# A different start order for a two-stage kernel: the first group alone up to its SSM block, and an input weight fetched ahead

## Chip, cores, metric

One NeuronCore of a Trainium2 (trn2) chip. The metric is device microseconds (us) of one execution; medians of several runs are given. "Warm" below means TensorE at its full clock, "cold" at half of it.

## The reference, cut to what matters

Two layers follow each other. All activations are float32; `moe_w_in` and `moe_w_out` arrive as float64.

```python
# gated linear attention, per batch b (4), head h (8), step t (768), head size 48
state = alpha[:, :, t, :, None] * state + einsum('bhd,bhe->bhde', k[:, :, t], v[:, :, t])
y[:, :, t] = einsum('bhd,bhde->bhe', q[:, :, t], state)
# gated SSM on x = y as (4, 768, 384)
proj = x @ w_in                       # (384, 1024): val | gate
h = exp(A_log) * h + val[:, t]        # scan over t
out = (silu(gate) * h) @ w_out        # (512, 384)
```

## The kernel before

The 4 x 768 steps are cut into N = 12 groups of 256 steps. A group passes through three generators; a `yield` ends a stage, and a schedule at the end decides which stage of which group is issued next. Each engine works through its instructions in the order in which they are issued.

- `front(n)`: transposes of alpha ("a"), scans V and P; transposes of q, product Q; of k, product K; scores `sc` and the masked copy A; K turned back (`tpk`, copies Kn). Five stages.
- `back(n)`: block states z and the running states S_n; y from inside a block; y from before it, then x_sb; x turned (xT). Four stages.
- `ssm(n)`: four blocks `pj` with scan `hh`, `sg` and `f`; two output products `o`. Six stages.

The float64 weights are turned into float32 by hand: 8 units of w_in and 4 of w_out. Step W(u) of `convert_weights` splits unit u and joins unit u-1.

```python
def split_unit(u):      # two ScalarE, two VectorE instructions, and on GpSimd:
    nc.gpsimd.tensor_scalar(out=ex, in0=ex, scalar1=896.0, scalar2=1151.0, op0=ALU.max, op1=ALU.min)
    nc.gpsimd.tensor_scalar(out=ex, in0=ex, scalar1=-896.0, scalar2=2.0 ** 23, op0=ALU.add, op1=ALU.mult)
def join_unit(u):
    nc.vector.scalar_tensor_tensor(out=ex, in0=hi, ...)
    nc.gpsimd.tensor_add(dst, dst, lo.bitcast(FP32))
    nc.gpsimd.tensor_mul(dst, dst, ex.bitcast(FP32))
def convert_weights():
    for u in range(len(units) + 1):
        if u < len(units):
            split_unit(u)
        if u > 0:
            join_unit(u - 1)
        yield

def back(n):            # (cut) first stage
    if not first:
        nc.gpsimd.tensor_mul(S_n[:, 0], S_end[0], ...)   # GpSimd, behind whatever W stands before it
    zv = block_states(s["Kn"], v_sb, ps_y)               # TensorE: z
    ...                                                  # VectorE: S_n, S_end from z
    yield

def ssm(n, ...):        # (cut) block cc needs units 2*cc (i = 0) and 2*cc + 1 (i = 1)
    for cc in range(NI):
        for i in range(2):
            for kk in range(NK):
                nc.tensor.matmul(pj[:, i, :], w_in[:, kk, i, ds(cc * C, C)], xT[:, kk, :], ...)
        # VectorE scan hh, ScalarE sg, VectorE f
        yield
```

The schedule of before, with `turn` the conversion for n < 3, and `old` and `new` the ssm of groups n-3 and n-2:

```python
for n in range(N + 3):
    # fr = front(n), ba = back(n - 1)
    step(fr); step(turn); step(ba); step(old); step(old); step(fr); step(turn); step(ba)
    # new = ssm(n - 2)
    step(new); step(fr); load(n + 2)          # n == 0: the rest of the weight fetches
    step(turn); step(ba); step(new); step(fr); step(ba); step(turn); step(new); step(fr); step(turn); step(new)
```

Of the kernel before, what the change touches and what calls it, by code (L numbers as in the profile page):

```python
# [18 lines left out]
def kernel(  # L19
# [38 lines left out]
    NI = DI // C  # L58
    N = B * NG
# [18 lines left out]
    def load_heads(dst, src, n, queue=nc.sync):  # L78

        b, g = divmod(n, NG)  # L80
        for c in range(G):
            rows = ds(g * GC + c * C, C)
            queue.dma_start(out=dst[:, c, :, 0:D], in_=src[b, :, rows, :].rearrange("h p d -> p h d"))  # L83

    def ssm(n, xT, prev_h, pool, ps_mm):

        b, g = divmod(n, NG)
        f = pool.tile([C, NI, GC], FP32, name="f")
        for cc in range(NI):
            pj = ps_mm.tile([C, 2, GC], FP32, tag="mm", name="pj")  # L90
            for i in range(2):
                for kk in range(NK):
                    nc.tensor.matmul(pj[:, i, :], w_in[:, kk, i, ds(cc * C, C)], xT[:, kk, :],  # L93
                                     start=(kk == 0), stop=(kk == NK - 1))
            hh = pool.tile([C, GC], FP32, tag=f"h{cc}", name="hh")
            nc.vector.tensor_tensor_scan(  # L96
                out=hh, data0=a_dec[:, cc:cc + 1].to_broadcast([C, GC]), data1=pj[:, 0, :],
                initial=prev_h[cc][:, GC - 1:GC] if g else 0.0, op0=ALU.mult, op1=ALU.add)
            prev_h[cc] = hh
            sg = pool.tile([C, GC], FP32, name="sg")  # L100
            nc.scalar.activation(sg, pj[:, 1, :], AF.Silu)  # L101
            nc.vector.tensor_mul(f[:, cc, :], sg, hh)  # L102
            yield
        for c in range(G):
            o = ps_mm.tile([C, DM], FP32, tag="mm", name="o")
            for cc in range(NI):
                nc.tensor.matmul(o, f[:, cc, ds(c * C, C)], w_out[:, cc, :],  # L107
                                 start=(cc == 0), stop=(cc == NI - 1))
            o_sb = pool.tile([C, DM], FP32, name="o_sb")
            nc.scalar.activation(o_sb, o, AF.Copy)  # L110
            nc.sync.dma_start(out=out[b, ds(g * GC + c * C, C), :], in_=o_sb)
            yield
# [9 lines left out]
    def block_states(Kn, v_sb, ps_y):  # L122

        z = ps_y.tile([C, NR, 512], FP32, tag="y", name="z")
        zv = z[:, :, 0:GP * D].rearrange("p r (g j e) -> p r g j e", g=G, e=D)
        for g in range(G):
            for j in range(NP):
                for r in range(NR):
                    for i in range(2):
                        rows, chs = ds(R * r, R), ds(DP * i, DP)  # L130
                        nc.tensor.matmul(zv[chs, r, g, j, :], Kn[rows, g, j, chs],
                                         v_sb[rows, g, 2 * j + i, :], start=True, stop=True,
                                         skip_group_check=True)
        return zv
# [32 lines left out]
    def features(x_sb, xT, ps_tp):  # L167

        for c in range(G):
            tp = ps_tp.tile([C, NK, C], FP32, tag="tp", name="tpx")  # L170
            for kk in range(NK):
                nc.tensor.transpose(tp[:, kk, :], x_sb[:, c, ds(kk * C, C)], ident)  # L172
            nc.scalar.activation(xT[:, :, ds(c * C, C)], tp, AF.Copy)

    def step(gen):
        if gen is not None:
            next(gen, None)


    def ranged(ctx):  # L180
        def pool(name, bufs, **kw):
            return ctx.enter_context(tc.tile_pool(name=name, bufs=bufs, **kw))
# [3 lines left out]
        p2 = pool("p2", 2)  # L186
# [6 lines left out]
        ps_mm = pool("ps_mm", 2, space=PS)  # L193
# [8 lines left out]
        vs, st, xs = {}, {}, {}  # L202

        def load(n, names="aqkv", queue=nc.sync):
            for name in names:
                if name == "v":
                    vs[n] = p3.tile([C, G, H, D], FP32, name="v_sb")
                dst = vs[n] if name == "v" else pads[n % NBUF][name]
                load_heads(dst, dict(a=alpha, q=q, k=k, v=v)[name], n, queue)
# [3 lines left out]
        units = []  # L213
# [8 lines left out]
        def fetch_unit(u, queue=nc.sync):  # L222
            dst, src = units[u]
            m, w = dst.shape[1:]
            bits = wst.tile([C, m, w, 2], U32, name=f"bits{u}")
            queue.dma_start(out=bits.rearrange("p a n two -> p a (n two)"), in_=src.bitcast(U32))  # L226
            words.append(bits)
# [24 lines left out]
# [7 lines that stand above are left out]
# [5 lines left out]
        prev_h = [None] * NI  # L264
# [75 lines left out]
        def back(n):  # L340

            s = st.pop(n)
            v_sb = vs.pop(n)
            first, last = n % NG == 0, n % NG == NG - 1
            S_n = p2.tile([C, GR, NP, D], FP32, name="S_n")
            if not first:
                nc.gpsimd.tensor_mul(S_n[:, 0], S_end[0], s["V"][:, :, 0:1].to_broadcast([C, NP, D]))  # L347
            zv = block_states(s["Kn"], v_sb, ps_y)
            S_end[0] = None if last else p2.tile([C, NP, D], FP32, name="S_end")
            for x in range(GR):  # L350
                src = zv[:, x % NR, x // NR]
                dst = S_n[:, x + 1] if x + 1 < GR else S_end[0]
                if first and x == 0:
                    nc.vector.tensor_copy(out=dst, in_=src)
                elif dst is not None:
                    nc.vector.tensor_add(dst, S_n[:, x], src)  # L356
            yield
            yv = values_inside(s["A"], v_sb, ps_y, p2)
            yield
            values_before(yv, s["Q"], S_n, first)  # L360
            x_sb = p2.tile([C, G, DM], FP32, name="x_sb")
            for i in range(2):
                nc.scalar.activation(x_sb.rearrange("p g (j i e) -> p i (g j) e", i=2, e=D)[:, i],
                                     yv[:, i].rearrange("p g j e -> p (g j) e"), AF.Copy)
            yield
            xs[n] = p2.tile([C, NK, GC], FP32, name="xT")
            features(x_sb, xs[n], ps_tp)
            yield

        ssms = {n: None for n in range(-3, N + 3)}  # L370
# [14 lines left out]
        load(0, "a")  # L385
        load(0, "q", nc.scalar)
        load(0, "k")
        fetch_unit(0)
        nc.scalar.dma_start(out=a_log, in_=moe_A_log.rearrange("(a p) -> p a", p=C))
        load(0, "v")  # L390
        fetch_unit(1)
        load(1, "aq")
        fetch_unit(2)
        load(1, "kv")
        for u in range(3, 6):
            fetch_unit(u)
        nc.scalar.activation(a_dec, a_log, AF.Exp)
        weights = convert_weights()

        def any_outside():  # L400
# [7 lines left out]
            nc.vector.tensor_reduce(out=w1, in_=wt, axis=mybir.AxisListType.X, op=ALU.max)  # L408
            nc.vector.tensor_scalar(out=flag, in0=w1, scalar1=0.0, scalar2=None, op0=ALU.is_gt)


        with tc.manual_schedule():
            for n in range(N + 3):
                fr = front(n) if n < N else None
                ba = back(n - 1) if 0 <= n - 1 < N else None
                old, new = ssms[n - 3], None
                turn = weights if n < 3 else None
                step(fr)
                step(turn)
                step(ba)  # L420
                step(old)
                step(old)
                step(fr)
                step(turn)
                step(ba)
                if 0 <= n - 2 < N:
                    new = ssms[n - 2] = ssm(n - 2, xs.pop(n - 2), prev_h, p2, ps_mm)
                step(new)
                step(fr)
                if n + 2 < N:  # L430
                    load(n + 2)
                if n == 0:
                    for u in range(6, len(units)):
                        fetch_unit(u)
                step(turn)
                step(ba)
                step(new)
                step(fr)
                step(ba)
                step(turn)  # L440
                step(new)
                step(fr)
                step(turn)
                step(new)
                if n == N:
                    any_outside()
                if n == N + 1:
                    outside = nc.values_load(flag[0:1, 0:1], min_val=0, max_val=1)
# [167 lines left out]
```

## Time and profile before

| | before |
|---|---|
| median of 4 runs | 374.15 us (373.93 to 374.33) |
| span of the profiled run | 372.8 us |
| TensorE busy | 325.8 us, 87% |
| VectorE, ScalarE, GpSimd busy | 54%, 29%, 15% |
| mean granted TensorE clock, as recorded | 0.975 |

In the profile PE is TensorE, PEld its weight loads, DVE VectorE, ACT ScalarE, POOL GpSimd and SP the engine that issues most DMAs. In the slices each digit is a busy share in tenths (9 is 90% or more), PEclk the granted TensorE clock in tenths; "out<-in xcount" names what a group of instructions writes and reads.

TensorE is full from about 66 us on. GpSimd is busy only 15% of the whole span, but nearly all of it lies in the first 70 us. The share of the span says nothing about that stretch.

Eight transposes of alpha took 1.94 us at 28.96, against 1.04 us at 87.48, and y took 3.65 us at 39.37, against 2.07 us at 96.07.

```profile
28.96 1.94 PE L294 MATMUL tp<-ident,a_pad 128*128 128x128 f32 x8 [7.17 <-POOL ex L240]
...
39.37 3.65 PE L145 MATMUL y<-v_sb,A 64*64 64x48 f32 x64 [1.60 <-DVE S_end L356]
```

### The profile page before, as it was taken

To read this page: it belongs to the slowest core of one execution; us is meant where nothing else is said; L and a number is where in the kernel's file an instruction comes from. 1 tells how busy PE (TensorE), PEld (TensorE's weight loads), DVE (VectorE), ACT (ScalarE), POOL (GpSimd) and SP (SyncE) were. 2 spreads that over 40 slices of the span, in tenths; PEclk is the share of its full clock that TensorE was granted. 3 is DMA by queue.
4 is the path that set the end of the run, shared out by engine and by line. 5 is a ranking of instruction groups with operands and counts; after the bars stand their busy time and mean duration, and the time that the engine had idled before them with its cause. 6 is when DMAs were issued, how large, how long until landed. Compare 5 with 4: busy or idle time off the path is not lost.

```text
span 372.8 us, 9626 instructions
## 1 busy us (share of the span) xinstructions
PE 325.8 (87%) x4233; PEld 265.6 (71%) x4233; DVE 200.5 (54%) x373; ACT 106.5 (29%) x231; POOL 56.8 (15%) x77
## 2 busy tenths in 40 slices
PE   2535851899999999999999999999999999999794
PEld 1425741787887886887887887878868868878582
DVE  3939785356557438348456555565484493403140
ACT  1414354221432323133223213223332231312111
POOL 4478898510000000000000000000000000000000
PEclk9999995599999999999999999999999999999999
DMA  9999992040470740911913704607401000010101
GB/s 132 212 220 190 303 171 47 2 86 2 105 111 2 154 60 3 179 36 41 145 30 80 134 2 100 115 3 130 85 2 44 2 16 30 2 45 0 38 7 50
DMA packets 107650, 29.02 MB, mean 78 GB/s; under 512 B 100944, under 2 KB 107088, under 8 KB 107600
## 3 DMA queue, kind: packets, MB, share of 16 engines
q1 hardware_dynamic: 104992, 27.93, 40.6%
q10 hardware_dynamic: 2608, 0.40, 0.9%
q8 instruction: 35, 0.57, 0.7%
q14 instruction: 15, 0.12, 0.1%
HBM read 23.60 MB, written 4.72 MB: 76 GB/s over the span
## 4 chain that ended last, share of the span: by engine, by line
PE 62%; DVE 23%; SPq 6%; issue 4%; POOL 2%; DMA 1%; ACT 1%; ACTq 0%; DVEq 0%; POOLq 0%
PE pj L93 35%; PE y L145 7%; DVE V L301 7%; DVE P L306 7%; PE o L107 4%; SPq L83 4%; PE y L163 4%; PE sc L331 3%; PE tp L294 3%; DVE S_n L356 3%; PE tpk L119 2%; PE tpx L172 2%; SPq L226 2%; DVE hh L96 2%; DMA bits<-in_moe_w_in_dram 1%
## 5 line engine op out<-in xcount | busy, mean ns | idle before, releaser
L93 PE MATMUL pj<-xT,w_in 128*128 128x256 f32 x576 | 136.1, 388 | 0.0
L93 PEld LDWEIGHTS pj<-xT,w_in 128*128 128x128 f32 x576 | 107.7, 193 | 14.6
L96 DVE TENSOR_TENSOR_SCAN hh<-a_dec,hh,pj 128x256 f32<-128x256 f32 x32 | 23.9, 747 | 78.2 <-PE pj L93 78.2
L107 PE MATMUL o<-w_out,f 128*128 128x384 f32 x192 | 65.0, 492 | 0.0
L101 ACT ACTIVATE sg<-pj 128x256 f32<-128x256 f32 x48 | 18.4, 383 | 130.9 <-DVE hh L96 130.9
L107 PEld LDWEIGHTS o<-w_out,f 128*128 128x128 f32 x192 | 35.5, 190 | 23.0 <-DVE f L102 0.5
L145 PE MATMUL y<-v_sb,A 64*64 64x48 f32 x768 | 28.0, 233 | 11.9 <-DVE S_end L356 11.2
L347 POOL TENSOR_TENSOR S_n<-S_end,V 128x192 f32<-128x192 f32 x8 | 4.1, 513 | 224.2 <-DVE S_end L356 224.2
L145 PEld LDWEIGHTS y<-v_sb,A 64*64 64x64 f32 x768 | 26.7, 149 | 15.1 <-issue 8.3
L306 DVE TENSOR_TENSOR_SCAN P<-tp,iV,bias 128x256 f32<-128x256 f32 x48 | 33.4, 738 | 0.8
L102 DVE TENSOR_TENSOR f<-sg,hh 128x256 f32<-128x256 f32 x48 | 20.4, 426 | 23.3 <-ACT sg L101 23.3
L301 DVE TENSOR_TENSOR_SCAN V<-tp,bias 128x256 f32<-128x256 f32 x48 | 30.1, 669 | 5.1 <-PE tp L294 5.1
L96 DVE TENSOR_TENSOR_SCAN hh<-a_dec,pj 128x256 f32<-128x256 f32 x16 | 11.0, 687 | 39.4 <-PE pj L93 39.4
L311 ACT ACTIVATE junk<-V,bias 128x1024 f32<-128x1024 f32 x12 | 13.8, 1148 | 52.7 <-DVE V L301 52.7
L294 PE MATMUL tp<-ident,a_pad 128*128 128x128 f32 x96 | 14.6, 300 | 15.6 <-POOL ex L240 7.2
L294 PE MATMUL tp<-ident,q_pad 128*128 128x128 f32 x96 | 15.5, 306 | 11.9 <-DVE P L306 7.7
L294 PEld LDWEIGHTS tp<-ident,a_pad 128*128 128x128 f32 x96 | 12.4, 154 | 17.4 <-POOL ex L240 7.5
L294 PEld LDWEIGHTS tp<-ident,q_pad 128*128 128x128 f32 x96 | 12.4, 157 | 16.4 <-issue 13.8
L240 POOL TENSOR_SCALAR ex<-ex 128x384 uint32<-128x384 uint32 x12 | 18.4, 1532 | 18.0 <-DVE ex L235 17.7
L331 PEld LDWEIGHTS sc<-Q,K 64*64 64x64 f32 x768 | 13.7, 144 | 4.3 <-issue 3.3
L334 DVE COPY_PREDICATED A<-mask,sc 128x512 f32<-128x512 uint8 x24 | 16.0, 721 | 1.1 <-PE sc L331 1.1
L322 DVE TENSOR_TENSOR K<-tp,V 128x512 f32<-128x512 f32 x24 | 15.5, 684 | 2.0 <-PE tp L294 2.0
(59 smaller groups left out, 315.6 us busy)
## 6 DMA issues: line engine op xcount, KB each, us to landing
a_pad<-in_alpha_dram SPq DMA_DIRECT2D x24, 192.0 KB, 4.7
k_pad<-in_k_dram SPq DMA_DIRECT2D x24, 192.0 KB, 5.1
v_sb<-in_v_dram SPq DMA_DIRECT2D x24, 192.0 KB, 5.0
out_dram<-o_sb SPq DMA_DIRECT2D x24, 192.0 KB, 2.1
q_pad<-in_q_dram SPq DMA_DIRECT2D x22, 192.0 KB, 5.0
bits<-in_moe_w_in_dram SPq DMA_DIRECT2D x8, 384.0 KB, 5.4
bits<-in_moe_w_out_dram SPq DMA_DIRECT2D x4, 384.0 KB, 6.1
q_pad<-in_q_dram ACTq DMA_DIRECT2D x2, 192.0 KB, 5.5
```

What stands on the lines that cost most here:

```text
L93: nc.tensor.matmul(pj[:, i, :], w_in[:, kk, i, ds(cc * C, C)], xT[:, kk, :], start=(kk == 0), stop=(kk == NK - 1))
L96: nc.vector.tensor_tensor_scan(out=hh, data0=a_dec[:, cc:cc + 1].to_broadcast([C, GC]), data1=pj[:, 0, :], initial=prev_h[cc][:, GC - 1:GC ...
L101: nc.scalar.activation(sg, pj[:, 1, :], AF.Silu)
L102: nc.vector.tensor_mul(f[:, cc, :], sg, hh)
L107: nc.tensor.matmul(o, f[:, cc, ds(c * C, C)], w_out[:, cc, :], start=(cc == 0), stop=(cc == NI - 1))
L145: nc.tensor.matmul(yv[rows, i, c, j, :], A[rows, i, c * NP + j, :], v_sb[rows, c, 2 * j + i, :], start=(c == 0 and j == 0), stop=False, sk ...
L240: nc.gpsimd.tensor_scalar(out=ex, in0=ex, scalar1=896.0, scalar2=1151.0, op0=ALU.max, op1=ALU.min)
L294: nc.tensor.transpose(tp[:, u, ds(c * C, C)], pad[name][:, c, 2 * j:2 * j + 2, :], ident)
L301: nc.vector.tensor_tensor_scan(out=V[:, 2 * jj + u, GC - 1::-1], data0=tp[:, u, ::-1], data1=bias[:, 1:2].to_broadcast([C, GC]), initial=1 ...
L306: nc.vector.tensor_tensor_scan(out=P[:, 2 * jj + u, :], data0=tp[:, u, :], data1=bias[:, 1:2].to_broadcast([C, GC]), initial=iV0[:, 2 * jj ...
L331: nc.tensor.matmul(scv[ds(R * r, R), i, c * NP + j, :], K[rows, j, steps], Q[rows, j, steps], start=True, stop=True, skip_group_check=True)
L334: nc.vector.copy_predicated(out=A[:, i].rearrange("p x t -> p (x t)"), mask=mask[:, ds(i * GP * R, GP * R)], data=sc[:, i])
```

## The change

Its intent: group 0 alone can reach its xT early. Then its pj blocks, TensorE work of some 11 us at full clock, can run in the holes that TensorE has while group 1 is at its scans and scores. For this the units of w_in must be there early, so they are fetched before group 1's inputs. The core of the diff (cut: comments and the branches that only keep other iterations as they were):

```diff
-        fetch_unit(0)
         nc.scalar.dma_start(out=a_log, ...)
         load(0, "v")
-        fetch_unit(1)
-        load(1, "aq")
-        fetch_unit(2)
-        load(1, "kv")
-        for u in range(3, 6):
+        for u in range(2 * NI):
+            fetch_unit(u)
+        load(1)
+        for u in range(2 * NI, len(units)):
             fetch_unit(u)
...
+            fr, ba = front(0), back(0)
+            for gen in (fr, fr, weights, fr, weights, fr, weights, fr, ba, weights, ba, ba, ba):
+                step(gen)
+            new = ssms[0] = ssm(0, xs.pop(0), prev_h, p2, ps_mm)
+            fr = front(1)
+            for gen in (fr, weights, new, fr, weights, new, fr, weights, weights, new, fr, weights, weights, new, fr):
+                step(gen)
+            load(2)
...
-            for n in range(N + 3):
+            for n in range(2, N + 3):
                 step(fr)
-                step(turn)
+                if n == 2:
+                    step(weights)
+                    step(weights)
                 step(ba)
...
-                if n + 2 < N:
-                    load(n + 2)
+                if n + 1 < N:
+                    load(n + 1)
...
+                step(old if n == 2 else new)     # n == 2: the o products of group 0, at two places
```

More of the change, by code (lines that the diff above doesn't have):

```diff
@@ L412, in ranged @@
         with tc.manual_schedule():
-            for n in range(N + 3):
-                fr = front(n) if n < N else None
-                ba = back(n - 1) if 0 <= n - 1 < N else None
-                old, new = ssms[n - 3], None
-                turn = weights if n < 3 else None
+            fr, ba = front(0), back(0)
[7 more added lines that the diff above has]
+            for n in range(2, N + 3):
+                fr = front(n) if n < N else None
+                ba = back(n - 1) if n - 1 < N else None
+                new = None
+                old = ssms[n - 3] if n > 2 else ssms[0]
+                if n == 2:
+                    early, old = None, old
                 step(fr)
-                step(turn)
+                if n == 2:
+                    step(weights)
+                    step(weights)
                 step(ba)
-                step(old)
-                step(old)
+                if n > 2:
+                    step(old)
+                    step(old)
                 step(fr)
-                step(turn)
+                if n == 2:
+                    step(weights)
+                    step(weights)
                 step(ba)
-                if 0 <= n - 2 < N:
+                if 2 < n < N + 2:
                     new = ssms[n - 2] = ssm(n - 2, xs.pop(n - 2), prev_h, p2, ps_mm)
@@ L429, in ranged @@
                 step(fr)
-                if n + 2 < N:
-                    load(n + 2)
-                if n == 0:
-                    for u in range(6, len(units)):
-                        fetch_unit(u)
-                step(turn)
+                if n + 1 < N:
+                    load(n + 1)
                 step(ba)
-                step(new)
+                step(old if n == 2 else new)
                 step(fr)
                 step(ba)
-                step(turn)
-                step(new)
+                step(old if n == 2 else new)
                 step(fr)
-                step(turn)
                 step(new)
```

## The prediction

> **What bounds the kernel now.** I read the page's 40 slices first (one slice is 9.3 us).
>
> ```profile
> PE   2535851899999999999999999999999999999794
> POOL 4478898510000000000000000000000000000000
> PEclk9999995599999999999999999999999999999999
> DMA  9999992040470740911913704607401000010101
> ```
>
> From slice 9 on TensorE is full; only the first 70 us have holes. TensorE is busy for 325.8 of 372.8 us, so 47 us are idle, nearly all in this head. There GpSimd works on the twelve units of float64 weights (eight of w_in, four of w_out), which are turned into float32, and the DMA engines are full for six slices. Slices 7 and 8 run at half the TensorE clock.
>
> Next the waits, longest first (total us, times, longest):
>
> ```profile
> PE y L145 <- DVE S_end L356: 11.2, 8, 5.4
> ACT bits L233 <- DMA bits<-in_moe_w_in_dram: 10.3, 3, 4.6
> DVE S_n L356 <- POOL S_n L347: 3.7, 1, 3.7
> ```
>
> ScalarE waits 10.3 us in three pieces for w_in to land. The longest single TensorE wait is 5.4 us, for the states of a group. The timeline shows what is behind it (start, duration):
>
> ```profile
> 59.55 0.34 DVE L235 TENSOR_SCALAR ex<-bits 128x384 uint32<-128x384 uint32 x1
> ...
> 59.97 1.52 POOL L240 TENSOR_SCALAR ex<-ex 128x384 uint32<-128x384 uint32 x1 [0.87 <-DVE ex L235]
> ...
> 61.58 0.51 POOL L241 TENSOR_SCALAR ex<-ex 128x384 uint32<-128x384 uint32 x1
> 62.05 1.00 POOL L249 TENSOR_TENSOR w_out<-w_out,bits 128x384 f32<-128x384 f32 x1
> 63.13 0.99 POOL L250 TENSOR_TENSOR w_out<-w_out,ex 128x384 f32<-128x384 f32 x1
> 64.08 0.51 POOL L347 TENSOR_TENSOR S_n<-S_end,V 128x192 f32<-128x192 f32 x1
> 64.63 1.13 DVE L356 TENSOR_TENSOR S_n<-S_n,z 128x192 f32<-128x192 f32 x3 [3.71 <-POOL S_n L347]
> ...
> 66.30 3.65 PE L145 MATMUL y<-v_sb,A 64*64 64x48 f32 x64 [5.43 <-DVE S_end L356]
> ...
> 69.88 5.07 PE L93 MATMUL pj<-xT,w_in 128*128 128x256 f32 x12
> ...
> 87.48 1.04 PE L294 MATMUL tp<-ident,a_pad 128*128 128x128 f32 x8
> ```
>
> One conversion step costs GpSimd 1.52 + 0.51 (split of a unit) + 1.00 + 0.99 (join of the unit before), 4.05 us from step to step. The state update S_n stands behind such a step in GpSimd's queue, VectorE behind S_n, TensorE behind VectorE. The first SSM product (pj) starts at 69.88, the a-transposes of group 3 at 87.48. From there a group takes some 26.2 us (the next group's begin near 113.5), with TensorE full. What the change does is therefore read at one point: when do group 3's a-transposes start?
>
> **What the Trainium skill says.** "TensorE: Matmul & The Clock Gate", Part 1 (What's actually happening): the array runs at half clock by default and after about one idle window of 3.4 us, and needs as long a busy stretch to get full speed. The trace agrees: y takes 3.65 us after that wait and 2.07 us at 96.07, a block of twelve pj 5.07 us at 69.88 and 2.86 at 76.83. The same page, Architectural detail: the queues of ScalarE, VectorE and GpSimd are strict FIFO. The trace agrees, S_n above starts only when the join ahead of it has ended; my argument rests on this. "DMA: Bandwidth & Descriptors", Specifications: transfers under 512 B miss line rate. The trace agrees: the loads of q, k, v and alpha (192 B rows, most of the 100944 packets under 512 B) move at 153 to 200 GB/s, stretches of weight units alone at 310 to 393.
>
> **The change part by part.** Arithmetic and instruction counts stay. Three things move.
>
> The fetch: load 0 (1.57 MB), then all eight w_in units (3.1 MB), then load 1, the w_out units, load 2. At the rates above I estimate load 0 in by 11 us, a unit every 1.5 us (w_in all in by 23), group 1's inputs by 30, w_out by 36. The step that waited for DMA at 20.94 and 26.93 no longer waits. This takes away the 10.3 us of DMA waits, but it only pays where the order of instructions lets conversion run.
>
> The order: conversion steps W0 to W3 stand among group 0's stages, W4 to W9 among group 1's, W10 to W12 in the iteration of group 2. I walk the queues with the durations of the trace. Group 0: scans end at 13.9, Q at 15.9 (as before), W0 16.7, K 18.1, W1 19.5, scores 20.3, A 21.7, W2 23.1, Kn copies 24.2, z 25.7, S_n 27.2, W3 28.7; y, cold, 27.3 to 31.0, its second part 32.6, x_sb 33.5, transposes and xT 35.0. GpSimd ends W3 near 31.6. Now the a-transposes of group 1 stand behind all that in TensorE's queue: they start at 34.6 (before: 28.96), the scans take 5.7 us to 40.9, and only then comes W4 on VectorE. So GpSimd stands still for about 10 us, 31.6 to 41.3, where before it ran almost without a gap from 28 to 64. Steps W4 to W12 are left.
>
> The ring that then forms: pj of block c needs two units joined by GpSimd; the scan hh, sg and f of block c stand on VectorE ahead of the next steps W. From 41.3: W4 joins unit 3 at 45.4; pj 0 (36 to 39) waits for VectorE and a table load on ScalarE, f 45.2; Q 46.5, W5, join at 50.9. pj 1 starts 45.4, cold after 4 us of idling: 5.0, hh, sg, f 1.6: 52.0; K 53.3; W6 starts, joins unit 5 at 57.8 (0.4 + 4.05); pj 2 cold to 62.8, f 64.4, A 65.9, W8 joins unit 7 at 70.4; pj 3 cold to 75.4, f 77.0. Only then can the Kn copies and group 2's transposes pass: scans from 77.6 to 83.3 (before: 53.96 to 59.6). Were pj warm all three times (2.8 instead of 5.0), this would be 76.7.
>
> Group 2's iteration: W10 and W11 both stand ahead of S_n, where before it was W10 alone. So S_n comes 0.4 + 2 x 4.05 + 0.5 = 9.0 us after the scans, VectorE's part of it 1.5 more: y starts 10.6 us after the scans (before 6.75), at 93.9. Then y 3.65 cold, k-transposes 2.0, y 1.5, o 2.8, scores 1.1, transposes 0.85, o 2.7, tpk 0.9, Kn 0.1: 15.6. Group 3's a-transposes start at 109.5 (warm case 103) against 87.48: 15.5 to 22 us later.
>
> From there nothing is won back. Group 3's iteration lacks the o products of group 0 (5.36 us), but they lay under the 5.7 us of scans that the q-transposes and y wait for; the hole stays and the iteration keeps its length. The later loads go out one iteration later (n+1 instead of n+2), but right behind the out stores, about 9 us into an iteration, and take about 8 us: landed by 19 of 26 us, hidden. The tail is the same. Sum: 374.3 + 15.5 to 22, middle about +19: **393 us**.
>
> **The rivals.** (1) The intended gain: pj of group 0 (11.2 us warm, 13.5 as it ran) fills holes of the head and the start of the full stretch comes forward, to perhaps 365 us. For it speak the 47 idle us and the vanished DMA waits. Against it speaks a floor: conversion can't go on before 41.3, W4 to W11 take GpSimd 8 x 4.05 = 32.4 us, S_n and VectorE 2.1, then 15.6 of TensorE: 91.4, 3.9 us later than before even with GpSimd never idle from there. (2) GpSimd nearly saturated: if VectorE runs ahead of GpSimd more than I think and the ring is loose, one lands near that floor, 378 to 382, called the same or just slower. For it: there are three ex buffers, so VectorE may be two units ahead; against it: W8 stands behind f of block 2 and that behind join 5, both in strict order. (3) TensorE stays cold in the whole head and the loads that go out later are not hidden: each group that waits 1 us gives 8 us more, 400 and above. Against it, 7 us of slack in my count of the loads.
>
> **Range and chances.** The warm and cold case give 390 and 396. Misjudged overlaps in the first 35 us and in the ring are worth perhaps 6 us each way, and the floor of 378 bounds the good side: 384 to 401. Faster by 2% (under 366.8) would need the floor to be wrong by 11 us: 0.03. Within 2% (to 381.8) means the loose ring: 0.08. Slower: 0.89.
>
> **What would show it.** Right, if in the changed profile: no wait of ScalarE for w_in; GpSimd idle for about 10 us between 31 and 42; the first pj near 36 and the fourth after 65, with idle TensorE and half clock between them; y of group 1 starting near 90 behind S_n, behind two joins; group 3's a-transposes at 103 to 110; 26 us per group from there on. Wrong, if GpSimd is busy throughout 41 to 75 (rival 2), if group 3's transposes begin before 88 (rival 1), or if the waits of the a-transposes for DMA recur in every group (rival 3).

## More of the kernel before

One more line of the waits (total us, times, longest) is needed for the comparison, how long GpSimd waits for VectorE to begin a conversion step:

```profile
POOL ex L240 <- DVE ex L235: 17.7, 9, 9.4
```

The longest of these, 9.4 us, is the wait for the first step.

## The result, and the profile after

The changed kernel takes 394.16 us (median of 4 runs, 393.64 to 394.39): **slower by 5.3%**, a ratio of 1.053 with an interval of 1.052 to 1.055. A ratio here is the mean time of one kernel's runs over that of the other's of the same rounds (those of the experiments leave out the first, profiled run), so it isn't quite the ratio of the medians quoted.

The slices of after (one is 9.8 us), to hold against those of before in the prediction:

```profile
PE   2659655609879999999999999999999999999894
POOL 4392687291000000000000000000000000000000
PEclk9975866856959999999999999999999999999999
DMA  9999950000490046093190380730904801010001
```

TensorE is full only from slice 13. GpSimd, which ran almost through in before, drops to 2 tenths in slice 4 (29 to 39 us) and again in slice 8 (69 to 79 us). The row of the clock shows several low pieces in the head, where that of before shows one; but the row of before misses low stretches (it has 9 in the first six slices, but the durations of before show half clock there too, at 28.96 and 39.37), so the two can't be compared by it. The DMA engines are done with their first rush in slice 6, so the data were there.

The waits of after:

```profile
POOL ex L240 <- DVE ex L235: 32.2, 6, 11.4
PE y L145 <- DVE S_end L356: 16.1, 8, 10.2
PE pj L93 <- POOL w_in L250: 11.4, 4, 4.3
```

GpSimd waits 32.2 us for VectorE to start conversion steps (17.7 before). TensorE has a wait it did not have: pj for joins of w_in, 11.4 us. Its wait for S_end grew from 11.2 to 16.1 us. The waits for weight DMAs, 10.3 us on ScalarE and 6.4 us on VectorE, are no longer in the list.

The timeline of after at the places that matter (start, duration, engine, what, idle time before and its cause):

```profile
33.40 1.94 PE L294 MATMUL tp<-ident,a_pad 128*128 128x128 f32 x8
...
40.55 1.49 POOL L240 TENSOR_SCALAR ex<-ex 128x384 uint32<-128x384 uint32 x1 [8.57 <-DVE ex L235]
...
40.83 1.46 PE L93 MATMUL pj<-xT,w_in 128*128 128x256 f32 x6
...
44.73 2.93 PE L93 MATMUL pj<-xT,w_in 128*128 128x256 f32 x6 [2.45 <-POOL w_in L250]
...
66.87 2.93 PE L93 MATMUL pj<-xT,w_in 128*128 128x256 f32 x6 [4.34 <-POOL w_in L250]
...
86.85 0.51 POOL L347 TENSOR_TENSOR S_n<-S_end,V 128x192 f32<-128x192 f32 x1
...
89.06 3.65 PE L145 MATMUL y<-v_sb,A 64*64 64x48 f32 x64 [10.20 <-DVE S_end L356]
...
104.49 1.14 PE L294 MATMUL tp<-ident,a_pad 128*128 128x128 f32 x8 [0.25 <-ACT Kn L120]
...
108.19 0.63 PE L294 MATMUL tp<-ident,q_pad 128*128 128x128 f32 x4 [1.47 <-issue]
...
111.02 1.09 PE L294 MATMUL tp<-ident,q_pad 128*128 128x128 f32 x4 [2.20 <-DVE P L306]
...
115.63 4.71 PE L93 MATMUL pj<-xT,w_in 128*128 128x256 f32 x12
...
132.87 1.04 PE L294 MATMUL tp<-ident,a_pad 128*128 128x128 f32 x8
```

Read from the top: group 1's a-transposes wait until group 0 is through. GpSimd has stood still for 8.57 us when it gets step W4. The second pj block comes in two halves, of which only the second waits for a join. The last half block of pj of group 0 starts at 66.87, after a wait for its weights. S_n of group 1 comes at 86.85 and y at 89.06, and group 3 begins at 104.49 (87.48 before). Group 4 begins at 132.87; in before it was 113.45:

```profile
113.45 1.04 PE L294 MATMUL tp<-ident,a_pad 128*128 128x128 f32 x8
```

That is the whole loss. From group 4's a-transposes to the end the two spans are alike: 372.8 - 113.45 = 259.35 us before and 392.7 - 132.87 = 259.83 us after. The head is 132.87 - 113.45 = 19.4 us longer.

### The profile page after: what moved, and what is told of

It is laid out like the page before. It is cut to its first block, busy times and chain, and to the rows that moved or that the text cites. A ratio compares the mean times of both kernels' runs of the same rounds, so it can differ in the third digit from the quotient of the medians. Undisturbed runs are those within 1.5% of the kernel's fastest.

```text
span 392.7 us, 9628 instructions
## 1 busy us (share of the span) xinstructions
PE 334.5 (85%) x4233; PEld 270.4 (69%) x4233; DVE 202.9 (52%) x373; ACT 107.1 (27%) x231; POOL 57.5 (15%) x77
## 4 chain that ended last, share of the span: by engine, by line
PE 63%; DVE 23%; POOL 5%; issue 4%; ACT 2%; DMA 1%; SPq 0%; ACTq 0%; POOLq 0%; DVEq 0%
PE pj L93 34%; PE y L145 8%; DVE P L306 7%; DVE V L301 7%; PE o L107 5%; PE tp L294 4%; PE y L163 4%; PE sc L331 3%; PE tpx L172 3%; PE tpk L119 2%; DVE S_n L356 2%; POOL ex L240 2%; DVE hh L96 2%; DMA a_pad<-in_alpha_dram 1%; ACT sg L101 1%
## 5 line engine op out<-in xcount | busy, mean ns | idle before, releaser
L93 PE MATMUL pj<-xT,w_in 128*128 128x256 f32 x576 | 143.2, 401 | 11.4 <-POOL w_in L250 11.4
L93 PEld LDWEIGHTS pj<-xT,w_in 128*128 128x128 f32 x576 | 111.4, 200 | 28.8 <-POOL w_in L250 13.1
L145 PE MATMUL y<-v_sb,A 64*64 64x48 f32 x768 | 29.6, 240 | 16.6 <-DVE S_end L356 16.1
L145 PEld LDWEIGHTS y<-v_sb,A 64*64 64x64 f32 x768 | 28.3, 157 | 19.6 <-issue 12.9
L102 DVE TENSOR_TENSOR f<-sg,hh 128x256 f32<-128x256 f32 x48 | 21.8, 453 | 24.6 <-ACT sg L101 24.6
L240 POOL TENSOR_SCALAR ex<-ex 128x384 uint32<-128x384 uint32 x12 | 18.5, 1538 | 32.7 <-DVE ex L235 32.2
L322 DVE TENSOR_TENSOR K<-tp,V 128x512 f32<-128x512 f32 x24 | 15.5, 683 | 3.4 <-PE tp L294 3.4
```

Of the source, the lines that this page charges most:

```text
L102: nc.vector.tensor_mul(f[:, cc, :], sg, hh)
L145: nc.tensor.matmul(yv[rows, i, c, j, :], A[rows, i, c * NP + j, :], v_sb[rows, c, 2 * j + i, :], start=(c == 0 and j == 0), stop=False, sk ...
```

## The experiments

The theory: the order of the queues costs the time, in three terms that add. (a) W4 (step 4 of the conversion) and its followers stand behind group 1's scans, GpSimd stands still, and pj then waits for joins. (b) S_n stands behind two joins. (c) The o products of group 0 left a hole that is there anyway and went to a place on the path. The main rivals were that the fetch order starves group 1, and that GpSimd's total conversion work bounds the head in any order.

The table has one row per kernel, in us from the start of the span of its profiled run, read from the timelines. Two runs of like code differ by up to 1.4 us here (compare the first column for after, e3, e4, e7). The last column is against before on the same chip in the same rounds: e1 to e4 ran on one chip (before at a median of 374.74), e5 to e8 on another (373.67), e9 in a third call (373.08). Since the chips differ a little, gains against after are worked out from ratios: the difference of the two ratios times 374.15 us. By the intervals of the ratios such a gain is uncertain by some 1 to 2 us. The intervals of all nine experiments exclude 1.

| kernel | scans of group 1 | scans of group 2 | y of group 1 | a-tp of group 3 | a-tp of group 4 | median time | ratio to before |
|---|---|---|---|---|---|---|---|
| before | 30.85 | 53.96 | 66.30 | 87.48 | 113.45 | 374.15 | 1 |
| after | 34.52 | 72.25 | 89.06 | 104.49 | 132.87 | 394.16 | 1.053 |
| e1 | 29.36 | 52.45 | 64.80 | 85.94 | 111.91 | 372.57 | 0.994 |
| e2 | 35.13 | 70.96 | 87.77 | 102.35 | 130.20 | 393.70 | 1.053 |
| e3 | 35.86 | 73.78 | 90.58 | 101.20 | 126.97 | 387.76 | 1.034 |
| e4 | 34.76 | 72.74 | 79.99 | 97.76 | 126.47 | 387.12 | 1.032 |
| e5 | 35.70 | 61.55 | 78.36 | 93.86 | 122.29 | 382.65 | 1.023 |
| e6 | 35.78 | 62.72 | 69.97 | 80.55 | 106.32 | 366.64 | 0.979 |
| e7 | 34.43 | 71.47 | 88.27 | 102.93 | 128.70 | 391.08 | 1.047 |
| e8 | 29.21 | 51.81 | 59.12 | 79.75 | 105.73 | 367.02 | 0.982 |
| e9 | 29.24 | 52.20 | 59.52 | 74.52 | 100.29 | 361.22 | 0.967 |

All kernels gave the correct result.

### e1 and e2: one half of the change at a time

e1 is the schedule of before with the fetch order of after:

```diff
 # before.py: the first hunk of the change, and
-                if n == 0:
-                    for u in range(6, len(units)):
-                        fetch_unit(u)
```

> The order of instructions of the kernel before, with the fetch order of the kernel after. Theory (the order of the queues costs the 20 us, the fetch does not): 366 to 373 us, the DMA waits of ScalarE and VectorE (10.3 and 6.4 us) gone and the head some us shorter; what is left is set by GpSimd's conversion and the S_n behind it. Rival (fetching w_in ahead of group 1's inputs starves group 1): 380 us or more, with the a-transposes of group 1 waiting for DMA.

e2 is the reverse, the schedule of after with units and inputs fetched in the order of before (units 3 to 11 in one piece).

> The order of instructions of the kernel after, with the fetch order of the kernel before (w_out fetched right after w_in). Theory: 393 to 397 us, as slow as the whole change, since units 2 and 3 land at most 2 us after their steps ask for them and group 1's scans stay where they are. Rival (the fetch is the cause): near 374 to 380 us.

Measured: e1 372.57 us, ratio 0.994 (0.991 to 0.997); e2 393.70 us, ratio 1.053 (1.047 to 1.060). So the order carries the whole loss, and the fetch alone is worth about half a per cent. (In e2 waits of ScalarE for weight DMAs remain, 5.7 us in two pieces, one of 3.9 us where at most 2 was expected; its time is that of after all the same.) That the fetch gains so little, where 10.3 us of ScalarE's DMA waits go, is shown by e1's timeline around step W4:

```profile
23.70 1.22 PE L294 MATMUL tp<-ident,a_pad 128*128 128x128 f32 x8 [1.93 <-ACT Kn L120]
...
25.76 0.36 DVE L235 TENSOR_SCALAR ex<-bits 128x384 uint32<-128x384 uint32 x1 [0.90 <-POOL w_in L250]
...
28.09 1.35 DVE L247 SCALAR_TENSOR_TENSOR ex<-bits,ex 128x384 uint32<-128x384 uint32 x1 [1.51 <-POOL ex L241]
...
29.36 1.26 DVE L301 TENSOR_TENSOR_SCAN V<-tp,bias 128x256 f32<-128x256 f32 x2
```

The a-transposes of group 1 now start at 23.70 instead of 28.96. But the scan stands on VectorE behind W4, and W4 waits for GpSimd: 0.90 us for a buffer that a join has to free, 1.51 us for the split before. The wait for the DMA has become a wait for GpSimd; the scan comes 1.5 us earlier, and the time falls by about as much (374.7 to 372.6).

### e3: the o products back under group 3's scans

```diff
-                step(old if n == 2 else new)
+                step(None if n == 2 else new)
 ...
-                step(old if n == 2 else new)
+                step(None if n == 2 else new)
```

Group 3's iteration then finds group 0's ssm not yet used up and takes both o products where before has them.

> After, with the o products of group 0 put back under group 3's scans, where the kernel before has them. Theory: they cost 5.5 us on the path in group 2's iteration and left a hole in group 3's, in which the TensorE clock fell to half (2.4 us more there): 386 us, with y of group 2 at 2.1 us instead of 3.65. Rival (work moved from one full place to another): 394 us.

Measured: 387.76 us, ratio 1.034 (1.029 to 1.038), 7.4 us less than after ((1.0533 - 1.0336) x 374.15). From group 2's scans to group 3's a-transposes it takes 27.4 us (101.20 - 73.78) instead of 32.2, and from group 3's to group 4's 25.8 instead of 28.4:

```profile
103.36 5.43 PE L107 MATMUL o<-w_out,f 128*128 128x384 f32 x16
109.59 2.07 PE L145 MATMUL y<-v_sb,A 64*64 64x48 f32 x64
```

The o products take 5.43 us under the scans, and y behind them runs at full clock, 2.07 us, where it took 3.65 in after.

### e7: more work in the same hole

The 2.4 us in group 3's iteration could still be due to something else that e3 moved. So nothing is moved here, and 16 matmuls are added:

```diff
+        def extra_products():
+            for c in range(G):
+                o = ps_mm.tile([C, DM], FP32, tag="mm", name="ox")
+                for cc in range(NI):
+                    nc.tensor.matmul(o, fs[0][:, cc, ds(c * C, C)], w_out[:, cc, :], ...)
 ...
+                if n == 3:
+                    extra_products()
```

> After, with 16 more matmuls: the o products of group 0 are formed a second time, into a PSUM tile that nobody reads, between z and the q-transposes of group 3's iteration. Nothing is taken away. Theory (that hole is time TensorE waits through anyway, and its clock falls to half in it): 392 us, 2.4 us less than after in spite of 5.4 us more work, with y of group 2 at 2.1 and the first pj block of group 1 at 2.9 us. Rival (the 2.4 us there are something else, say late loads): 394 to 399 us.

Measured: 391.08 us, ratio 1.047 (1.045 to 1.049), 2.4 us less than after, with 5.4 us more TensorE work. The lines of group 3's iteration:

```profile
105.08 5.43 PE L416 MATMUL ox<-w_out,f 128*128 128x384 f32 x16
111.31 2.07 PE L148 MATMUL y<-v_sb,A 64*64 64x48 f32 x64
113.31 2.86 PE L96 MATMUL pj<-xT,w_in 128*128 128x256 f32 x12
```

Group 3's iteration is 25.8 us long (128.70 - 102.93; 28.4 in after). The 2.6 us are the clock, which the trace records as 0.50 from 112 to 116 us in after and as 1.00 from 111.3 to 116 us in e7: y is 1.6 us and the first pj block 1.8 us shorter, while y starts 0.8 us later in its iteration (8.4 us after the a-transposes, 7.5 in after).

### e4: S_n ahead of the conversion steps

```diff
                 step(fr)
-                if n == 2:
-                    step(weights)
-                    step(weights)
                 step(ba)
+                if n == 2:
+                    step(weights)        # W10; W11 behind the next front stage, W12 behind the one after
```

> After, with conversion steps 10 to 12 behind the state update S_n of group 1 instead of 10 and 11 ahead of it. Theory: y of group 1 starts 2 to 3 us after the scans instead of 11; the o products then wait for the last join, so 7 us are won: 387 us (385 to 389). Rival (GpSimd's whole conversion work bounds the head, order or no order): 392 to 394 us.

Measured: 387.12 us, ratio 1.032 (1.028 to 1.036), 8.0 us less than after.

```profile
79.99 3.65 PE L145 MATMUL y<-v_sb,A 64*64 64x48 f32 x64 [0.78 <-DVE S_end L356]
...
91.25 0.91 PE L107 MATMUL o<-w_out,f 128*128 128x384 f32 x2 [1.12 <-POOL w_out L250]
```

y comes 7.3 us after group 2's scans begin instead of 16.8, and 1.6 us after they end. Part of this is given back: the o products now wait for the last joins of w_out (0.87 and 1.12 us), as the theory had it.

### e5: conversion steps 4 and 5 ahead of group 1's scans

```diff
-            for gen in (fr, fr, weights, fr, weights, fr, weights, fr, ba, weights, ba, ba, ba):
+            for gen in (fr, fr, weights, fr, weights, fr, weights, fr, ba, weights, ba, weights, ba, ba, weights):
 ...
-            for gen in (fr, weights, new, fr, weights, new, fr, weights, weights, new, fr, weights, weights, new, fr):
+            for gen in (fr, weights, new, fr, weights, new, fr, weights, new, fr, weights, new, fr):
```

> After, with conversion steps 4 and 5 moved ahead of group 1's scans (between the stages of group 0's back), and the later ones spread one to a block. Theory: GpSimd's 8.6 us of standing still at 32 to 40 us go, pj no longer waits long for joins, group 2's scans start near 60 instead of 72 us: 382 us (379 to 386). Rival (the DMA engines or VectorE's own work bound this stretch): 391 to 394 us.

Measured: 382.65 us, ratio 1.023 (1.020 to 1.026), 11.5 us less than after. The edit does two things, W4 and W5 come early and W6 to W9 stand one to a block instead of in pairs; what each of them brought was not separated. GpSimd's slices in e5:

```profile
POOL 4299694820000000000000000000000000000000
```

The low slice at 29 to 39 us is gone, pj waits for a join once, for 1.9 us in all (11.4 in after), group 2's scans begin at 61.55 instead of 72.25, and the 10.7 us between reach group 3 in full (93.86 against 104.49).

### e6: all three moves

The edits of e3, e4 and e5 together.

> After with all three moves: o products back under group 3's scans, S_n ahead of the conversion steps, steps 4 and 5 early. Theory: the three terms add up (12 + 7 to 9 + 8, partly the same time): group 3's a-transposes near 78 to 80 us, 365 us (362 to 370), faster than the kernel before. Rival (the three terms are one and the same wait): 380 us or more.

Measured: 366.64 us, ratio 0.979 to before (0.976 to 0.982). Group 3's a-transposes come at 80.55, just past the 78 to 80 expected. One by one the moves are worth 7.4 + 8.0 + 11.5 = 26.9 us, together 27.7: within the error of the ratios they add. So the three terms account for the loss of 20 us and for nearly 8 more, by which this version beats before (its interval ends at 0.982, so the gain is sure but may be under 2%). The slices:

```profile
PE   2558777599999999999999999999999999998894
POOL 4299877380000000000000000000000000000000
```

TensorE is full from slice 9 (73 us on, at 9.2 us a slice).

### e8: what before loses itself

Before has one conversion step ahead of S_n of group 1. e8 is e1 with that one behind it:

```diff
                 step(fr)
-                step(turn)
+                if n < 2:
+                    step(turn)
                 step(ba)
+                if n == 2:
+                    step(turn)
```

> The order of the kernel before with the new fetch order (as in e1), and the first conversion step of group 2's iteration moved behind S_n. Theory (S_n behind a join costs the kernel before 4 to 5 us too): 367 to 369 us. Rival (GpSimd's total work bounds the head): 372 us as e1.

Measured: 367.02 us, ratio 0.982 (0.980 to 0.984), 4.6 us less than e1 by the ratios. y of group 1 starts at 59.12 after a wait of 0.39 us, where e1 waited 5.44:

```profile
59.12 3.65 PE L145 MATMUL y<-v_sb,A 64*64 64x48 f32 x64 [0.39 <-DVE S_end L356]
```

### e9: the intent of the change, at another place

In e8 TensorE idles under group 2's scans, and xT of group 0 is ready before. So two pj blocks go there, and the other two to the next two places:

```diff
                 if n == 2:
                     step(turn)
+                    early = ssms[0] = ssm(0, xs.pop(0), prev_h, p2, ps_mm)
+                    step(early)
+                    step(early)
 ...
+                if n == 2:
+                    new = early
-                if 0 <= n - 2 < N:
+                if 1 <= n - 2 < N:
 ...                                       # and for n == 2 the last two step(new) are left out
```

> e8 with the intent of the change put in at another place: the first two pj blocks of group 0 stand behind z of group 1, under group 2's scans, where TensorE waits for 7 us in e8, and the other two at the next two places. No step of the conversion moves. Theory (what counts is whether the moved work lies in a hole that is there anyway and holds up no conversion step): 5.6 us of pj leave the full stretch, and with the clock kept up y takes 2.1 instead of 3.65 us: 359 us (356 to 363). Rival (the end of group 2's iteration is set by VectorE and GpSimd, so pj moved forward wins nothing): 366 to 368 us as e8.

Measured: 361.22 us, ratio 0.967 to before (0.963 to 0.972), a little slower than the 359 expected.

```profile
50.91 5.45 PE L93 MATMUL pj<-xT,w_in 128*128 128x256 f32 x24
...
59.52 2.07 PE L145 MATMUL y<-v_sb,A 64*64 64x48 f32 x64 [0.88 <-DVE S_end L356]
...
62.31 2.83 PE L93 MATMUL pj<-xT,w_in 128*128 128x256 f32 x12 [0.72 <-ACT sg L101]
```

Two blocks run in 5.45 us under the scans, y at full clock. The third block waits 0.72 us for sg of the first to free its PSUM buffer. Group 3 begins 5.2 us before e8's (74.52 against 79.75). This is the fastest kernel of the study.

## Why the prediction was right

The predicted 393 us stands against 394.2. The direction holds, and so do the main steps of the mechanism; that the number is so close is partly luck, since two errors cancel. Step by step:

- **The slices.** The prediction read slices 7 and 8 as the stretch at half clock. The row says so, but the durations show half clock in earlier work of TensorE too (28.96 and 39.37 above). This did no harm, because the walk through the queues used measured durations.
- **Fetch.** Right. No wait for weight DMAs is left in after, and e1 shows the fetch alone worth half a per cent; the trace of e1 adds that GpSimd takes over the role of the DMA.
- **GpSimd stands still behind group 1's scans.** Predicted about 10 us, 31.6 to 41.3; measured 8.57 us, 31.98 to 40.55. e5 shows that it matters: 11.5 us.
- **The ring of joins, pj, f and the next W.** Right in kind, too long in size. The first pj starts at 35.13 (36 predicted). But the cold case had group 2's scans begin at 77.6 us; they begin at 72.25, near the warm case's 71 (76.7 at their end). The failed term is "pj of block c needs two units joined": it was counted as if no part could start before both. The trace has the block in two halves; the first six matmuls of block 1 start at 40.83 and only the other six, at 44.73, wait for the join. So a block costs the ring some 2.9 us at half clock and not 5.0. Half a block at half clock happens to last as long as the 2.8 us of the warm case for a whole one, so that case met the time for another reason than its own.
- **S_n behind two joins.** Predicted 10.6 us from the end of the scans to y; measured 11.1 (77.95 to 89.06). e4 shows it.
- **From y to group 3's a-transposes.** Predicted 15.6 us, measured 15.4. Group 3 begins at 104.49, 17.0 us later than before, inside the predicted 15.5 to 22.
- **"The hole stays and the iteration keeps its length."** This is a step that failed. The hole stays, as predicted, so moving the o products out of it won nothing there. But the iteration does not keep its length: 28.4 us instead of 26.0. With two idle stretches of 1.47 and 2.20 us around four short transposes, the clock falls to half, and y and a pj block pay for it. The prediction knew the clock gate and used it for other places, and forgot it in this one. e7 shows the clock to be the cause. These 2.4 us are missing from the sum. Group 3, on the other hand, begins 1.8 us before the middle of the predicted 15.5 to 22, mostly since the ring was shorter than the mean of the warm and the cold case (72.25 against 74.3). The two errors cancel, which is why the middle value of 19 met the measured 20 so closely.
- **Later loads and the tail.** Right: group 4 to the end takes 259.8 us and took 259.4.

The rivals: the intended gain was not to be had in this order of steps; e9 collects it at another place. In e6 the pj blocks stand where the change put them and wait only 3.1 us for joins, yet it ends only level with e8, which has none of them early (366.64 and 367.02 us; group 3 at 80.55 and 79.75). So e6's lead over before is no sign that this place for them pays. GpSimd's total work does not bound after's head: e6 does the same conversion work and is 27.7 us faster. Half clock is part of the loss (e7: 2.4 us in one iteration), and in the ring it was not separated from the waits by a run of its own; that share stays open.

## What to carry to other kernels

Work moved into holes of one engine is judged by what it drags along in the queues of the others: each engine takes its instructions in the order of issue, so a short instruction (here S_n, 0.51 us) behind a long helper task costs the whole task, and a helper task (here the weight conversion) behind a chain that waits stands still. Before moving anything, place the helper's steps where no short link of the main chain stands behind them and where they never wait for the main chain; then look for the hole. And a hole that some other latency keeps open should be left filled: emptying it gains nothing and can let TensorE's clock fall.

## What the Trainium skill lacked or had wrong

- "TensorE: Matmul & The Clock Gate", Why this matters for your kernels, advises against idle gaps of more than about 3 us between bursts. In after the clock fell to half although no gap in group 3's iteration reached that: 1.47 and 2.20 us, with 0.63 us of transposes between (four q-transposes took 0.63 us, then 1.09). The granted clock is recorded as 1.00 up to 109.0 us and as 0.50 from 109.25 us, only some 2.5 us after the last matmul of z.
- The same page, Part 4 (PE-mode transpose), says that the full clock does not engage for transposes. The transposes of these kernels, which the trace records as matmuls with an identity (whether the page's transpose mode was on, it does not say), do run at two speeds: eight took 1.94 us cold (33.40 in after) and 1.04 us warm (132.87), the latter right behind dense matmuls. Whether transposes alone bring the full clock or keep it no run here was made to show.
- "GPSIMD Engine Reference", Performance versus the Vector engine, Elementwise, names the operation of a measured time for a two-tensor add only. Here the operator decided, at one and the same shape of 128 x 384 elements: max and min with two constants took mostly 1.49 us, add and multiply with two constants 0.51 us, and a two-tensor add 1.00 us.
- No page warns of a pattern that cost much here: a short GpSimd instruction of the main chain behind a helper's long ones. It cost before 4.6 us (e1 to e8) and after 8.0 us (e4), although the TensorE page does say that GpSimd's queue is strict FIFO.
